# One core, FFT mixing then swish MLP: closing block ordered per output part, first filter group over two queues, evacuations of `a`, `y` and tables shared out

## Chip, cores, metric

One core of a Trainium2 chip. The metric is the device time of one execution in microseconds (us) in the undisturbed ("fast") state, with a granted TensorE clock of 0.998 to 1.0. The profiled span is shorter than the device time of the same execution, by 2.05 us in the first trace and by 1.76 to 3.37 us over all executions; so part of the scatter of device times lies outside the span (one execution of e7 took 785.17 us with a span of 781.8).

## The reference

```python
X = np.fft.rfft(x, axis=1)                         # x: (8, 3008, 256)
Y = X * (filt_r + 1j * filt_i)[None]               # filters: (1505, 256)
x = np.fft.irfft(Y, n=3008, axis=1).reshape(-1, 256)   # 24064 tokens
h = x @ w_in                                       # 256 -> 2048
out = (h / (1 + np.exp(-beta * h))) @ w_out        # 2048 -> 256
```

## The kernel before

The FFT is factored (3008 = 47 x 64) into matmuls with tables that are made on the chip. Sequence 0 is transformed in the set-up (up to 36 us); the seven others are transformed in *units* placed between the steps of the MLP. A step is one filter block of one block of 512 tokens: the h matmul, the activation `gT` on ScalarE, and two steps later the `acc` matmuls. A *turn* of `a` is six transposes into one PSUM tile and their evacuation; an *inner unit* reads `a` back, multiplies it by the filter on VectorE and transforms it on. `S`, `NK`, `NFB` are 3008, 24 and 16. The parts that matter:

```python
def evac(dst, src, on_act, scale=None):            # PSUM -> SBUF
    if on_act: nc.scalar.activation(dst, src, ACT.Copy, ...)
    else:      nc.vector.tensor_copy(dst, src)     # cut

FG = [(g * KG, KG) for g in range(NG)]             # four groups of six filter rows
for h in range(2):                                 # group 0 on POOL's queue, right behind x
    for f, at in ((filt_r, 0), (filt_i, M)):
        load_filter(fri, f, at, *FG[0], gp)[h]()
for part in FG[1:]:                                # the others on SP's queue
    ...

def turn_a(i, on_act):                             # six transposes into one PSUM tile, then one evacuation
    pb = opsum.tile([P, 3, D], BF16, name="pb", tag="acc")
    for e in range(3):
        for dc in range(NDC):
            nc.tensor.transpose(pb[:, e, dc * P : (dc + 1) * P], a_t[...], ident[:])
    evac(a2s[-1][:, 3 * (i % 2) : 3 * (i % 2) + 3, :], pb[:], on_act)
turn_a(0, False); turn_a(1, True)

# placing of units over the steps (place(first, last, units, per step))
place(2, 14, uz(1, True)); place(15, 29, uz(2))    # turns and y of groups 1 and 2
units = uz(3, True); place(20, 24, units[:2], per=2); place(34, 58, units[2:])
at = place(25, 58, u23(1), per=2, gap=2)           # inner units of sequence 1

# closing block: four output parts of 128 tokens, each with its own PSUM tile
todo = [(gT, fb, tb) for tb in range(nch)]
...
on_act = h == 0 and i < 6 or last and h % 2 == 0
evac(ost[:, c : c + per, :], a[:], on_act)
eng = nc.scalar if last and h >= 2 else nc.sync
store(t0 + h * per * P, per * P, ost[:, c : c + per, :], eng)
```

Of the kernel before, what the change touches and what calls it, by code (L numbers as in the profile page):

```python
# [9 lines left out]
P = 128  # L10
# [3 lines left out]
F32 = mybir.dt.float32  # L14
BF16 = mybir.dt.bfloat16
# [11 lines left out]
M = 64  # L27
H = M // 2
NK = 24
J = 32  # L30
KG = 6
NG = NK // KG
# [7 lines left out]
def kernel(  # L40
# [10 lines left out]
    nc = tc.nc  # L51

    B, S, D = x.shape
# [5 lines left out]
    NDC = D // P  # L59
    NFB = FF // P  # L60
    NP = 2 * N1
    KP = 4 * NK
    TB = 512
# [15 lines left out]
    a2pool = pool("a2pool", 5)  # L79
    pqpool = pool("pqpool", 3)  # L80
    vpool = pool("vpool", 4)
    gpool = pool("gpool", 4)
# [24 lines left out]
    def evac(dst, src, on_act, scale=None):  # L107
        if on_act:
            nc.scalar.activation(dst, src, ACT.Copy, scale=1.0 if scale is None else scale)  # L109
        elif scale is None:  # L110
            nc.vector.tensor_copy(dst, src)  # L111
        else:
            nc.vector.tensor_scalar_mul(dst, src, scale)  # L113
# [48 lines left out]
    setup = sp.enter_context(tc.tile_pool(name="setup", bufs=1))  # L162
# [43 lines left out]



    FG = [(g * KG, KG) for g in range(NG)]
    for h in range(2):  # L210
        for f, at in ((filt_r, 0), (filt_i, M)):
            load_filter(fri, f, at, *FG[0], gp)[h]()
    for part in FG[1:]:
        for h in (1, 0):
# [47 lines left out]
    NH = NK // 2  # L262
    us = []
    for h in range(2):
        u = setup.tile([P, NH, M], I32, name="u", tag=f"u{h}")
# [5 lines left out]
        )  # L271
        nc.vector.tensor_scalar(u[:], u[:], TURN - 1, None, ALU.bitwise_and)
        us.append(u)
    rs = [setup.tile([P, NH, M], F32, name="r", tag=f"r{h}") for h in range(2)]

    def t2_part(h, part):
        u, r = us[h], rs[h]
        ks_ = slice(h * NH, (h + 1) * NH)
        if part == 0:
            nc.scalar.activation(  # L280
                t2[:, ks_, 2, :], u[:], ACT.Sin, scale=TWO_PI / TURN, bias=pi[:]
            )
        elif part == 1:
            nc.scalar.activation(r[:], u[:], ACT.Abs, scale=1.0 / TURN, bias=half[:])
        else:
            for cols, sgn, b in ((slice(0, H), -1.0, hp), (slice(H, M), 1.0, hm)):
                nc.scalar.activation(
                    t2[:, ks_, 1, cols], r[:, :, cols], ACT.Sin, scale=sgn * TWO_PI, bias=b[:]
                )
# [104 lines left out]
    a2s = []  # L394

    def turn_a(i, on_act):
        if i % 2 == 0:
            a2s.append(a2pool.tile([P, KG, D], BF16, name="a2", tag="a2"))
        pb = opsum.tile([P, 3, D], BF16, name="pb", tag="acc")
        for e in range(3):  # L400
            k1 = 3 * i + e
            for dc in range(NDC):
                nc.tensor.transpose(
                    pb[:, e, dc * P : (dc + 1) * P],
                    a_t[:, dc, k1, :, :].rearrange("p j a -> p (j a)"),
                    ident[:],
                )
        evac(a2s[-1][:, 3 * (i % 2) : 3 * (i % 2) + 3, :], pb[:], on_act)

    def load_win(h):  # L410
        fs = slice(h * FF // 2, (h + 1) * FF // 2)
# [180 lines left out]
    rest = []  # L592
    for i in range(2 * NDC):
# [1 line left out]
            [P, 4, P], F32, name="ps4", tag="acc" if i % 2 else "f"  # L595
        )
        rest += last_z(0, i, i % 2 == 1, own)
    for go in rest:
        go()

    sp.close()

# [95 lines left out]
    NBLK = (TOK + TB - 1) // TB  # L698
# [4 lines left out]
    def place(a, z, units, clear=False, per=1, gap=0):  # L703
        last_at = a
        for n, go in enumerate(units):
            at = a + (z - a) * n / max(1, len(units) - 1)
            at = max(int(at), last_at + gap if n else last_at)
            if clear and (at % NFB < 2 or at % NFB > 13):
                at += (2 - at) % NFB
            while len(plan.get(at, ())) >= per:  # L710
                at += 1
            plan.setdefault(at, []).append(go)
            last_at = at
        return last_at

    def u1(b, act=False):
        def unit(i):
            def go():
                if i == 0:
                    start(b)  # L720
                s1(b, i, act and i % 2 == 1)

            return go

        return [unit(i) for i in range(J // 2)]

    def u23(b):
        return [lambda i=i: s23(b, i) for i in range(NK // 2 + VLAG)]
# [4 lines left out]
    def uz(g, act=False):  # L733
        return [lambda i=i: turn_z(g, i) for i in range(2)] + [
            lambda i=i: last_z(g, i, act) for i in range(2 * NDC)
        ]
# [21 lines left out]

        return [go]

    place(2, 14, uz(1, True))
    place(15, 29, uz(2))
    units = uz(3, True)
    place(20, 24, units[:2], per=2)
    place(34, 58, units[2:])
# [2 lines left out]
    if B > 1:  # L768
        units = u1(1, True)
        place(3, 8, units[: J // 4], per=2)  # L770
        place(10, 10, uf(0, JG), per=9)
        at = place(9, 14, units[J // 4 :], per=9)
        place(at + 1, at + 1, [lambda: a2_read(1)] + uf(JG, NK), per=9)
        place(14, 20, ut(4), per=2)
        at = place(25, 58, u23(1), per=2, gap=2)
        assert at < 60
        place(60, 60, [lambda: zz_read(1)], per=9)
        place(67, 79, u4(1), per=2)
    if B > 2:
        place(36, 36, ux(2), per=9)  # L780
        at = place(54, 68, u1(2, True), per=3)
        assert at < 75
        place(75, 75, [lambda: a2_read(2)], per=9)
    for b in range(2, B):
        a = first_step[b - 1]
# [32 lines left out]
                c0 += n  # L818

    blk = {}  # L820
    LAG = 2
    for s in range(len(steps) + LAG):
        if s < len(steps):
            i, fb = steps[s]
            t0 = i * TB
            tn = min(TB, TOK - t0)
            hps = hpsum.tile([P, TB], F32, name="hps", tag="hps")
            pos = t0
            while pos < t0 + tn:
                b, n0 = divmod(pos, S)  # L830
                ln = min(S - n0, t0 + tn - pos)
                if s == 0:
                    ln = min(ln, CLS - n0 % CLS)
                for dc in range(NDC):
                    nc.tensor.matmul(  # L835
                        hps[:, pos - t0 : pos - t0 + ln],
                        lhsT=win_sb[:, dc, fb * P : (fb + 1) * P],
                        rhs=ys[b][:, dc, n0 : n0 + ln],
                        start=(dc == 0),
                        stop=(dc == NDC - 1),  # L840
                    )
                pos += ln
            gT = gpool.tile([P, TB], BF16, name="gT", tag="gT")
            nc.scalar.activation(  # L844
                gT[:, :tn], hps[:, :tn], ACT.Silu, scale=beta_sb[:, fb : fb + 1]
            )
            blk[s] = gT
        if s in plan:
            for go in plan[s]:
                go()  # L850
        if s >= LAG:
            i, fb = steps[s - LAG]
            t0 = i * TB
            tn = min(TB, TOK - t0)
            nch = tn // P
            gT = blk.pop(s - LAG)

            last = i == NBLK - 1
            if fb == 0 and not last:
                acc = [opsum.tile([P, 2, D], F32, name="acc", tag="acc") for _ in range(2)]  # L860
            elif fb == 0:
                acc = [
                    (fpsum if h % 2 else opsum).tile(
                        [P, 1, D], F32, name="acc", tag="f" if h % 2 else "acc"
                    )
                    for h in range(nch)
                ]
            per = acc[0].shape[1]


            todo = [(gT, fb, tb) for tb in range(nch)]
            if fb == 0:
                todo, late = todo[: nch // 2], todo[nch // 2 :]
            elif fb == 1:
                todo[nch // 2 : nch // 2] = late
            for g_, f_, tb in todo:
                nc.tensor.matmul(  # L877
                    acc[tb // per][:, tb % per, :],
                    lhsT=g_[:, tb * P : (tb + 1) * P],
                    rhs=wout_sb[:, f_, :],  # L880
                    start=(f_ == 0 and tb % per == 0),
                    stop=(f_ == NFB - 1),
                    skip_group_check=True,
                )
            if fb == NFB - 1:
                for h, a in enumerate(acc):
                    if h * per % 2 == 0:
                        ost = ostp.tile([P, 2, D], F32, name="ost", tag="ost")
                    c = h * per % 2
                    on_act = h == 0 and i < 6 or last and h % 2 == 0  # L890
                    evac(ost[:, c : c + per, :], a[:], on_act)
                    eng = nc.scalar if last and h >= 2 else nc.sync
                    store(t0 + h * per * P, per * P, ost[:, c : c + per, :], eng)


# [28 lines left out]
```

## Time and profile before

| | device time |
|---|---|
| median of 3 | 783.36 us (781.89 to 783.63) |
| the profiled execution | 784.25 us, span 782.2 us |

The page and the chain of waits are in the prediction. One more stretch is needed later: the timeline of the kernel before at the first turn of `a`. Columns of a timeline: start, duration, engine, line, operation, output<-input, shape, count, and in brackets the idle time of the engine ahead of it and what ended it.

```profile
15.32 0.84 PE L403 MATMUL pb<-ident,a_t 128*128 128x128 bf16 x12
15.67 0.64 ACT L287 ACTIVATE t<-r,hm 128x384 bf16<-128x384 f32 x1
15.86 0.56 DVE L111 COPY a<-pb 128x768 bf16<-128x768 bf16 x1 [0.60 <-PE pb L403]
16.20 0.81 ACT L109 ACTIVATE a<-pb 128x768 bf16<-128x768 bf16 x1
16.47 0.38 PE L446 MATMUL ps<-a,t 128*128 128x256 bf16 x2 [0.31 <-DVE a L111]
16.90 0.87 ACT L109 ACTIVATE t<-pt 128x128 bf16<-128x128 bf16 x2
20.08 0.38 PE L472 MATMUL psz<-t,pb_t 128*128 128x128 bf16 x4 [0.21 <-ACT a L109]
```

Twelve transposes (two turns) run in one go; VectorE takes the first turn whole, ScalarE the second, and the first product follows 0.80 us after ScalarE's table step from `hm` has started. Call the start of that step **hm**, the first `psz` matmul **psz**. From hm to psz ScalarE has one thing after another to do: 4.41 us.

### The profile page before, as it was taken

How to read it: one execution, taken by the hardware profiler on the slowest of the kernel's cores; microseconds unless marked ns; L12 is line 12 of the kernel's file. 1: busy time of each engine (PE TensorE's matmuls, PEld its weight loads, DVE VectorE, ACT ScalarE, POOL GpSimd, SP SyncE). 2: the span in 40 equal slices, each digit the busy share in tenths (PEclk: the TensorE clock that was granted, in tenths of full speed). 3: DMA queues.
4: the chain of work that ended last, by engine and by line, in shares of the span. 5: the costliest groups of instructions: out<-in, count | busy, mean ns of one | idle time of the engine just before them, and what ended most of it. 6: DMA issues, size and time to landing. Idle time of an engine off the chain costs nothing.

```text
span 782.2 us, 15445 instructions
## 1 busy us (share of the span) xinstructions
PE 766.8 (98%) x6012; PEld 548.4 (70%) x6108; DVE 393.0 (50%) x644; ACT 594.5 (76%) x921; POOL 142.5 (18%) x145
## 2 busy tenths in 40 slices
PE   8999999999999999999999999999999999999997
PEld 5867667766777666876668766787677776776664
DVE  7847846646446563474636746277453751401001
ACT  6887887886678867787677876778767787677775
POOL 6522501320013100231002410034000430000000
PEclk9999999999999999999999999999999999999999
DMA  9978663517801286022941248312451114100101
GB/s 184 248 186 229 157 210 132 137 58 206 218 28 68 86 205 181 28 95 92 199 154 47 77 132 186 126 67 77 137 180 55 48 68 128 55 28 32 51 28 54
DMA packets 84185, 91.46 MB, mean 117 GB/s; under 512 B 4498, under 2 KB 74276, under 8 KB 83154
## 3 DMA queue, kind: packets, MB, share of 16 engines
q1 hardware_dynamic: 81008, 73.95, 30.7%
q0 software_dynamic: 2816, 16.26, 10.6%
q8 instruction: 48, 0.79, 0.4%
q10 hardware_dynamic: 288, 0.26, 0.1%
q14 instruction: 25, 0.20, 0.1%
HBM read 57.16 MB, written 46.66 MB: 133 GB/s over the span
## 4 chain that ended last, share of the span: by engine, by line
PE 94%; DVE 1%; ACT 1%; issue 1%; DMA 1%; POOL 0%; DVEq 0%; POOLq 0%
PE acc L877 43%; PE hps L835 38%; PE ps L626 3%; PE ps L551 3%; PE ps L674 2%; PE ps L648 2%; DMA xg<-in_x_dram 1%; PE psz L472 0%; DVE q_t L660 0%; ACT a L109 0%; PE pz L543 0%; DVE q_t L663 0%; DVE qb_t L455 0%; DVE p_t L659 0%; ACT a_t L109 0%
## 5 line engine op out<-in xcount | busy, mean ns | idle before, releaser
L844 ACT ACTIVATE gT<-hps,beta_sb 128x512 bf16<-128x512 f32 x752 | 516.0, 687 | 173.5 <-PE hps L835 152.1
L877 PE MATMUL acc<-wout_sb,gT 128*128 128x256 bf16 x3008 | 451.4, 272 | 3.0
L835 PE MATMUL hps<-y,win_sb 128*128 128x512 bf16 (+8 forms) x1636 | 427.4, 350 | 0.5 <-ACT gT L844 0.3
L877 PEld LDWEIGHTS <-gT 128*128 128x128 bf16 x3008 | 285.7, 98 | 128.1 <-ACT gT L844 0.2
L835 PEld LDWEIGHTS <-win_sb 128*128 128x128 bf16 x1730 | 165.0, 98 | 24.7 <-issue 0.6
L664 POOL TENSOR_TENSOR v_t<-p_t,q_t 128x512 bf16<-128x512 f32 x84 | 106.6, 1269 | 387.8 <-DVE q_t L663 381.6
L111 DVE COPY ost<-acc 128x512 f32<-128x512 f32 (+1 forms) x88 | 56.2, 677 | 192.8 <-PE acc L877 188.8
L111 DVE CAST a<-ps 96x512 bf16<-96x512 f32 x96 | 65.9, 687 | 86.2 <-PE ps L626 85.7
L113 DVE TENSOR_SCALAR y<-ps 128x376 bf16<-128x376 f32 (+1 forms) x119 | 63.8, 544 | 61.2 <-PE ps L551 61.2
L659 DVE TENSOR_TENSOR p_t<-ps,frr 128x512 f32<-128x512 f32 x84 | 58.1, 691 | 30.0 <-PE ps L648 28.0
L663 DVE TENSOR_TENSOR q_t<-ps,fri 64x512 f32<-64x512 f32 x84 | 58.3, 694 | 1.2
L660 DVE SCALAR_TENSOR_TENSOR q_t<-ps,fri 64x512 f32<-64x512 f32 x84 | 57.5, 684 | 1.1
L551 PEld LDWEIGHTS <-zz 96*128 96x128 bf16 x512 | 35.3, 97 | 28.9
L109 ACT ACTIVATE z<-ps 128x512 bf16<-128x512 f32 x84 | 49.5, 589 | 0.1
L626 PE MATMUL ps<-xg,t 94*96 94x512 bf16 x112 | 41.9, 381 | 0.7
L551 PE MATMUL ps<-t,zz 96*128 96x94 bf16 x448 | 36.7, 204 | 1.1
L674 PE MATMUL ps<-v_t,t 128*128 128x256 bf16 x168 | 32.1, 273 | 0.6 <-DVE q_t L663 0.6
L648 PE MATMUL ps<-a,t 128*128 128x256 bf16 x168 | 32.1, 273 | 0.1
L120 POOL DMA_DIRECT2D xg<-in_x_dram x22 | 12.1, 551 | 100.8 <-PE acc L877 96.8
L648 PEld LDWEIGHTS <-t 128*128 128x128 bf16 x168 | 15.8, 98 | 14.4
L626 PEld LDWEIGHTS <-t 94*96 94x96 bf16 x112 | 13.6, 123 | 11.9
L674 PEld LDWEIGHTS <-t 128*128 128x128 bf16 x168 | 16.1, 98 | 7.4 <-DVE q_t L663 1.3
(118 smaller groups left out, 191.6 us busy)
## 6 DMA issues: line engine op xcount, KB each, us to landing
out_dram<-ost SPq DMA_DIRECT2D x80, 256.0 KB
d<-a SPq DMA_DIRECT2D x28, 384.0 KB
a<-d SPq DMA_DIRECT2D x28, 384.0 KB
d<-z SPq DMA_DIRECT2D x28, 384.0 KB
zz<-d SPq DMA_DIRECT2D x28, 384.0 KB
xg<-in_x_dram POOLq DMA_DIRECT2D x6, 1280.0 KB, 10.1
frr<-in_filt_r_dram SPq DMA_DIRECT2D x12, 256.0 KB
out_dram<-ost SPq DMA_DIRECT2D x18, 128.0 KB
```

The source lines that it names most:

```text
L111: nc.vector.tensor_copy(dst, src)
L113: nc.vector.tensor_scalar_mul(dst, src, scale)
L551: nc.tensor.matmul(ps[:, e, :NP], lhsT=zz[:, jj + e, dc * P : (dc + 1) * P], rhs=tab[:], start=True, stop=True,)
L626: nc.tensor.matmul(ps[:KP], lhsT=t1[:], rhs=s["x"][:, 2 * i : 2 * i + 2, :], start=True, stop=True)
L648: nc.tensor.matmul(ps[:, e, :], lhsT=t2[:, k0 + e, 3:5, :].rearrange("p c k -> p (c k)"), rhs=s["a2"][g][:, kk + e, :], start=True, stop=True,
L659: nc.vector.tensor_tensor(p_t[:], ps[:], frr[:, ks_, :], ALU.mult)
L663: nc.vector.tensor_tensor(q_t[:M], ps[M:P], fri[M:P, ks_, :], ALU.mult)
L664: nc.gpsimd.tensor_tensor(v_t[:], p_t[:], q_t[:], ALU.add)
L674: nc.tensor.matmul(ps[:, e, :], lhsT=t3[:, k0 + e, :], rhs=v_t[:, e, :], start=True, stop=True)
L835: nc.tensor.matmul(hps[:, pos - t0 : pos - t0 + ln], lhsT=win_sb[:, dc, fb * P : (fb + 1) * P], rhs=ys[b][:, dc, n0 : n0 + ln], start=(dc ...
L844: nc.scalar.activation(gT[:, :tn], hps[:, :tn], ACT.Silu, scale=beta_sb[:, fb : fb + 1])
L877: nc.tensor.matmul(acc[tb // per][:, tb % per, :], lhsT=g_[:, tb * P : (tb + 1) * P], rhs=wout_sb[:, f_, :], start=(f_ == 0 and tb % per = ...
```

## The change

The intent: let the first product start earlier (split evacuation, split filter load), fill two small waits of TensorE, and let only one of four output parts be stored after the last matmul.

```diff
-    FG = [(g * KG, KG) for g in range(NG)]
+    FG = [(0, 2), (2, KG - 2)] + [(g * KG, KG) for g in range(1, NG)]
@@ turn_a, inside the loop over e, after the transposes of one e
-        evac(a2s[-1][:, 3 * (i % 2) : 3 * (i % 2) + 3, :], pb[:], on_act)
+            if i == 0 and e > 0:
+                ks_ = slice(0, 2) if e == 1 else slice(2, 3)
+                evac(a2s[-1][:, ks_, :], pb[:, ks_, :], e == 2)
+        if i > 0:
+            evac(a2s[-1][:, 3 * (i % 2) : 3 * (i % 2) + 3, :], pb[:], on_act)
@@ units
-    for go in rest:
-        go()
-    place(2, 14, uz(1, True))
-    place(15, 29, uz(2))
+    place(0, 0, rest, per=9)
+    place(1, 14, uz(1, True))
+    place(15, 29, uz(2, True))
-        at = place(25, 58, u23(1), per=2, gap=2)
+        units = u23(1)
+        place(20, 53, units[: NK // 2], per=2)
+        at = place(55, 58, units[NK // 2 :], per=2)
-        at = place(54, 68, u1(2, True), per=3)
+        at = place(52, 66, u1(2, True), per=3)
@@ closing block (gT of its last seven filter blocks kept in other pools: cut)
+            if last and fb >= NFB - 7:
+                kept += todo[nch // 2 :]
+                todo = todo[: nch // 2]
+                if fb == NFB - 1:
+                    kept.sort(key=lambda e: e[2])
+                    todo = kept[:4] + todo + kept[4:]
-                    on_act = h == 0 and i < 6 or last and h % 2 == 0
+                    on_act = h == 0 and i < 6 or last and h in (0, 3)
-                    eng = nc.scalar if last and h >= 2 else nc.sync
+                    eng = nc.scalar if last and h == 2 else nc.sync
```

Cut too: the set-up tile `r` becomes a single buffer.

More of the change, by code (lines that the diff above doesn't have):

```diff
@@ L273 @@
         us.append(u)
-    rs = [setup.tile([P, NH, M], F32, name="r", tag=f"r{h}") for h in range(2)]
+    r = setup.tile([P, NH, M], F32, name="r", tag="r")
     def t2_part(h, part):
-        u, r = us[h], rs[h]
+        u = us[h]
         ks_ = slice(h * NH, (h + 1) * NH)
@@ L820 @@
     blk = {}
+    kept = []
     LAG = 2
@@ L842 @@
                 pos += ln
-            gT = gpool.tile([P, TB], BF16, name="gT", tag="gT")
+            if i == NBLK - 1 and NFB - 7 <= fb < NFB - 3:
+                gT = vpool.tile([P, TB], BF16, name="gT", tag="v_t")
+            elif i == NBLK - 1 and NFB - 3 <= fb < NFB - 1:
+                gT = a2pool.tile([P, KG, D], BF16, name="gT", tag="a2")
+                gT = gT[:, :NDC].rearrange("p a d -> p (a d)")
+            else:
+                gT = gpool.tile([P, TB], BF16, name="gT", tag="gT")
             nc.scalar.activation(
```

## The prediction

> **What bounds the kernel now.** The time before is 783.36 us (median of 3, 781.89 to 783.63); the profiled span is 782.2 us. I read the page's busy shares and chain first, then the chain in order of time, then the timeline where the chain leaves TensorE.
>
> ```profile
> PE 766.8 (98%) x6012; PEld 548.4 (70%) x6108; DVE 393.0 (50%) x644; ACT 594.5 (76%) x921; POOL 142.5 (18%) x145
> ...
> PE 94%; DVE 1%; ACT 1%; issue 1%; DMA 1%; POOL 0%; DVEq 0%; POOLq 0%
> ```
>
> TensorE carries 94% of the chain. Its busy share alone says little, because matmuls overlap, so I took starts instead: in the main loop a 128x512 matmul starts 0.217 us after the one before it, a 128x256 one 0.109 us. Adding columns / 2.4 GHz + 2.5 ns over all matmul starts, every gap above this rate after 33 us is either exactly one 512-column matmul (a missing record) or one of these: 0.35, 0.22, 0.10, 0.14 and 0.15 us between 33 and 36 us, 0.51 at 37.3, 0.48 at 75.0, 0.45 at 85.2 and 0.06 at 112. From 113 us to the last matmul at 776.4 TensorE never waits, but for 0.24 us at the very end. The change leaves the number of matmuls alone (6,108 in both programs). So only three stretches can give anything: the set-up up to 37 us, the two waits near 75 and 85 us, and the tail.
>
> The set-up, from the chain in order of time:
>
> ```profile
> 15.30 1.01 ACT t L287 x2
> 16.31 0.70 ACT a L109
> 17.01 0.76 ACT t L109 x2
> 17.77 0.85 ACT t3b L109 x2
> 18.62 1.42 ACT a L109 x2
> 20.08 0.61 PE psz L472 x8
> ```
>
> ScalarE runs from 11.65 to 20 us without a gap, and each of its evacuations frees a PSUM buffer that TensorE wants. From 20.08 to 30.7 us TensorE itself has no gap, and VectorE's products follow it at the same pace. A shift of ScalarE before 20 us therefore shifts everything behind it.
>
> The waits of TensorE after the set-up, from the timeline:
>
> ```profile
> 37.31 0.59 PE L835 MATMUL hps<-y,win_sb 128*128 128x512 bf16 x2 [0.34 <-ACT gT L844]
> ...
> 75.03 0.39 PE L674 MATMUL ps<-v_t,t 128*128 128x256 bf16 x2 [0.32 <-DVE q_t L663]
> ...
> 85.22 0.39 PE L674 MATMUL ps<-v_t,t 128*128 128x256 bf16 x2 [0.28 <-DVE q_t L663]
> ```
>
> The first waits for the first activation, the other two for VectorE to finish reading a PSUM buffer (its product of the unit just before).
>
> The tail, from the timeline:
>
> ```profile
> 776.40 0.66 ACT L109 ACTIVATE ost<-acc 128x256 f32<-128x256 f32 x2 [0.38 <-PE acc L877]
> 776.51 0.76 DVE L111 COPY ost<-acc 128x256 f32<-128x256 f32 x2 [11.88 <-PE acc L877]
> 777.09 2.40 ACTq L796 DMA_DIRECT2D out_dram<-ost  x2
> ```
>
> All four output parts finish within 0.33 us (the last four matmuls start 776.08 to 776.42). The second store on ScalarE's queue is issued at 777.53 but takes 1.96 us to issue; its data lands at 780.7 to 781.22, and the span ends 0.97 us later.
>
> **What the Trainium skill says.** "Perfetto Trace Analysis", Identifying the Most-Contended Engine, warns that matmul occupancy is no measure of how near TensorE is to its limit; the trace agrees (98% busy, weight loads 70%), hence the start-to-start reading. "TensorE: Matmul & The Clock Gate", Back-to-back issue gap, gives N/2.4 + 2.5 ns (216 ns at N = 512) for an isolated matmul and 131 ns sustained; this trace has 217 ns in a sustained stream, so the first form holds here. "DMA: Bandwidth & Descriptors", Anatomy of one DMA, puts about 2 us of fixed cost on a DMA, mostly the receipt of the write; the last stores here land 1.6 to 1.9 us after issue on fifteen of sixteen engines, and 3.5 to 3.7 us on the sixteenth. "Runtime: NRT & Kernel Launch", Instruction fetch mechanics, says instructions come in 16 KiB blocks over a DMA queue; the trace has 48 such packets, the last from 777.7 to 779.1 us, just before the sixteenth engine delivers and while the slow store is being issued.
>
> **The change, part by part.**
>
> *First turn of a.* The first evacuation (128x768, VectorE, 0.56 us) becomes 128x512 on VectorE plus 128x256 on ScalarE. VectorE may begin two transposes earlier (2 x 0.056 = 0.11 us) and is shorter by about a third of its streaming part (estimate 0.13 us), so the first product can come some 0.25 us earlier. But ScalarE gets one more instruction in its gapless stretch. A 128x256 evacuation there costs 0.38 us, at a pitch of 0.28 us (the two at 776.40 and 776.68). The second product needs the table evacuated after it (TensorE waited for that at 17.82), so 20.08 becomes about 20.36: **+0.28 us**.
>
> *Filter group 0.* Before, its four loads on POOL's queue landed at 14.40, 15.21, 15.99 and 16.85 us, just ahead of the first product at 17.03. Without the split the earlier product would meet the load. Now a third of the bytes follow x (landing estimate 14.9: 1.1 us for 256 KB at the measured 3.04 us for 768 KB after x at 13.81), the rest starts on SP at 12.4. Total bytes are the same, so the rest should land near 17.1, before the second product at about 18. **0 us**, enabling only. Groups 1 to 3 keep their place in the byte stream.
>
> *Rest of y after the first activation, group 1's turn one step earlier.* In the order of the changed program eight transposes (8 x 0.056 = 0.45 us) now stand where TensorE waited 0.51 us at 37.31; 0.06 stays. The 128x240 evacuation on ScalarE moves between the first two activations (estimate 0.26 us of pitch), so the fourth step waits about 0.2 us. 0.51 becomes 0.26: **-0.25 us**.
>
> *Units of sequence 1 spread and y of group 2 on ScalarE.* The inner units stood every 2 to 3 steps from step 25; they now stand every 3 steps from step 21. One unit costs VectorE 0.69 + 0.68 + 0.69 = 2.06 us, a step about 1.1 us, so each unit is read before the next wants its buffer; four 0.55 us evacuations leave VectorE too. ScalarE has room: 6.5 to 8.4 of 10 us busy between 50 and 80 us, and back-to-back activations start every 0.58 to 0.65 us. Both waits should go: **-0.93 us**.
>
> *But the first unit now comes early.* It reads the transposed data of sequence 1:
>
> ```profile
> 54.67 0.31 SPq L631 DMA_DIRECT2D d<-a  x1
> ...
> 57.99 1.77 SPq L638 DMA_DIRECT2D a<-d  x4
> ```
>
> The last store of the transposition is issued at 54.67, the reads at 57.99; the first tile's sixteenth increment comes at 61.24. Nothing in that chain moves. In TensorE time the unit stands 23.89 + 0.43 us after the first h matmul (column sums of the changed program); 36.2 + 0.3 + 24.3 = 60.8. The data comes at 61.3: **+0.5 us**. Late in the stretch (steps 53 to 56), units, sequence 2's first matmuls and evacuations crowd the same three PSUM buffers; the dependences show margins of about 0.1 us: **+0.1 us**.
>
> *Tail.* Holding back half of the products of the last seven filter blocks lets the last h matmuls run at ScalarE's pace (about 0.69 us a step instead of 0.87, five steps), then twelve products follow the last activation instead of four. The work is the same; the waits (0.24 before, about 0.4 after) nearly cancel, so TensorE ends where it did. But parts 0, 1, 2 end 1.2, 1.1 and 0.76 us before the last matmul, so their evacuations and stores run beside it. Only part 3 is left: matmul, 0.3 us to ScalarE, which first issues part 2's store (0.40 us), so evacuation from +0.5 to +0.9 us, store issued on SP at about +0.9, that is at 777.3 instead of 777.53. On undisturbed engines it lands 1.75 us later (779.1), on the one busy with the instruction fetch until 779.1 at about 780.3 to 780.9 instead of 781.22. **-0.6 us** (0 to -2).
>
> Sum: 0.28 + 0 - 0.25 - 0.93 + 0.5 + 0.1 - 0.6 = -0.9; 783.36 - 0.9 = **782.5 us**.
>
> **Rivals.**
> 1. *The early unit eats the gain.* If the transposed data comes later than 61.3, each late microsecond stands in TensorE's queue one to one. SP's queue is in order and crowded there (eight loads behind). For: nothing speeds this chain. Against: step 21, not 20, since two units already fill step 20. It would give 783 to 784.
> 2. *The instruction fetch decides the tail.* If it still falls on the last store, the tail gives nothing: 783.1. If the store's packets avoid it, landing at 779.1 gives -2: 781.1.
> 3. *The split turn really gains.* If ScalarE has slack that I do not see, the earlier first product would carry through to 32 us: -0.25 instead of +0.28, total 782.0. The gapless chain speaks against it.
>
> **Range and chances.** The path effects are each below 1 us; runs of one kernel alone differ by 1.7 us. Low end 780.9: best tail, no early-unit wait; high end 784.0: rival 1 with an empty tail. A change of 2% is 15.7 us; no stretch offers that, and none of the added waits could lose it. Faster by over 2%: 0.01; within 2%: 0.98; slower: 0.01.
>
> **What would show it.** First psz matmul at 20.3 to 20.4 rather than 20.08; the first h matmul later by as much; no 0.5 us wait after the second h step; a new wait of the first unit's weight load or matmul for the read-back near 61; no wait for VectorE products at 70 to 90; matmul work ending near the same time, and the last store's issue under 0.5 us. I am wrong if the set-up ends earlier, if a wait over 1 us appears near 61 or 95, or if anything between 120 and 760 us changes.

## The result, and the profile after

| | before | after |
|---|---|---|
| median | 783.50 us (6 runs, 781.89 to 783.79) | 783.49 us (6 runs, 783.42 to 784.04) |
| ratio | | 1.0005, interval 0.9992 to 1.0018: same |

A ratio here compares one kernel's fast runs with the other's fast runs of the same rounds, and is not exactly the ratio of the medians or of the means (e5: 1.0013, by the means 1.0017). The page of the changed kernel, busy times and chain:

```profile
PE 772.4 (99%) x6108; PEld 548.5 (70%) x6108; DVE 390.8 (50%) x640; ACT 595.8 (76%) x926; POOL 142.9 (18%) x145
...
PE 95%; ACT 2%; DVE 1%; DMA 1%; issue 0%; DVEq 0%; ACTq 0%; POOL 0%; POOLq 0%; SPq 0%
```

TensorE carries the chain as before. The six further microseconds of busy PE are no change: the first trace has 6,012 matmul records, this one all 6,108. VectorE has four instructions fewer and ScalarE five more, as the change intends. Now the same stretch as shown for before, in the timeline of the changed kernel:

```profile
14.82 0.62 ACT L287 ACTIVATE t<-r,hm 128x384 bf16<-128x384 f32 x1
14.88 0.42 DVE L111 COPY a<-pb 128x512 bf16<-128x512 bf16 x1 [1.02 <-PE pb L403]
15.35 0.61 PE L403 MATMUL pb<-ident,a_t 128*128 128x128 bf16 x8 [0.51 <-DVE a L111]
15.66 1.15 ACT L109 ACTIVATE a<-pb 128x256 bf16<-128x256 bf16 x2 [0.21 <-PE pb L403]
15.80 0.38 PE L451 MATMUL ps<-a,t 128*128 128x256 bf16 x2
16.70 0.87 ACT L109 ACTIVATE t<-pt 128x128 bf16<-128x128 bf16 x2
19.88 0.38 PE L477 MATMUL psz<-t,pb_t 128*128 128x128 bf16 x4 [0.21 <-ACT a L109]
```

Three things stand here. psz is earlier in absolute time (19.88, not 20.08), but hm is earlier still (14.82, not 15.67): from hm to psz it is 5.06 us, 0.65 more. TensorE's fifth transpose waits 0.51 us for VectorE: the last third of the turn goes into the *same PSUM tile* as the part that VectorE is reading. And the row of 1.15 us on ScalarE is two evacuations (the 128x256 part, then the next turn's 128x768) where before there was one. The first product, for whose sake all this was done, starts 0.98 us after hm (15.80 - 14.82); before it was 0.80.

Where the schedule of the units was changed, the timeline of the changed kernel near 61 and 76 us:

```profile
61.29 0.39 PE L651 MATMUL ps<-a,t 128*128 128x256 bf16 x2 [0.32 <-DMA a<-d]
...
75.05 0.59 ACT L109 ACTIVATE ost<-acc 128x512 f32<-128x512 f32 x1
75.08 0.33 PE L556 MATMUL ps<-t4b,zz 96*128 96x94 bf16 x4
...
75.53 0.69 ACT L857 ACTIVATE gT<-hps,beta_sb 128x512 bf16<-128x512 f32 x1
75.89 0.38 PE L651 MATMUL ps<-a,t 128*128 128x256 bf16 x2
76.10 0.49 ACT L109 ACTIVATE y<-ps 128x376 bf16<-128x376 f32 x1
...
76.65 0.39 PE L677 MATMUL ps<-v_t,t 128*128 128x256 bf16 x2 [0.37 <-ACT y L109]
```

The wait for the read-back of sequence 1 is there, as predicted (0.49 us by the starts of the matmuls). The wait for VectorE at 85 us is gone, the one at 75 is not gone: it has turned into a wait for ScalarE. `y` of group 3 is ready at 75.4 (matmul L556), but ScalarE first evacuates an output part (75.05) and makes a `gT` (75.53), and the next inner unit needs the PSUM buffer that `y` is in: 0.53 us.

The tail, in the timeline of the changed kernel:

```profile
774.46 2.49 PE L897 MATMUL acc<-wout_sb,gT 128*128 128x256 bf16 x20
775.79 0.38 ACT L109 ACTIVATE ost<-acc 128x256 f32<-128x256 f32 x1 [0.38 <-PE acc L897]
775.90 0.76 DVE L111 COPY ost<-acc 128x256 f32<-128x256 f32 x2 [11.21 <-PE acc L897]
776.20 1.78 SPq L802 DMA_DIRECT2D out_dram<-ost  x3
776.68 0.37 ACTq L802 DMA_DIRECT2D out_dram<-ost  x1
777.24 0.38 ACT L109 ACTIVATE ost<-acc 128x256 f32<-128x256 f32 x1 [1.07 <-PE acc L897]
```

And in the timeline of the kernel before, in a second trace of it (a comment line moves its lines by one), because the first is not typical, as the next section shows:

```profile
774.55 1.61 PE L878 MATMUL acc<-wout_sb,gT 128*128 128x256 bf16 x12
775.87 0.66 ACT L110 ACTIVATE ost<-acc 128x256 f32<-128x256 f32 x2 [0.37 <-PE acc L878]
775.98 0.76 DVE L112 COPY ost<-acc 128x256 f32<-128x256 f32 x2 [11.88 <-PE acc L878]
776.28 0.82 SPq L797 DMA_DIRECT2D out_dram<-ost  x2
776.56 0.88 ACTq L797 DMA_DIRECT2D out_dram<-ost  x2
```

In the changed kernel three parts are evacuated or under way when the last matmul (776.68) starts, and one store is left; before, the first evacuation begins as the last matmul starts (775.87 and 775.89), and all four stores come after it.

### The profile page after: what moved, and what is told of

It reads as the page before. It is cut to its first block, busy times and chain, and to the rows that moved or that the text cites. A ratio compares the mean times of both kernels' runs of the same rounds, so it can differ in the third digit from the quotient of the medians.

```text
span 781.4 us, 15550 instructions
## 1 busy us (share of the span) xinstructions
PE 772.4 (99%) x6108; PEld 548.5 (70%) x6108; DVE 390.8 (50%) x640; ACT 595.8 (76%) x926; POOL 142.9 (18%) x145
## 4 chain that ended last, share of the span: by engine, by line
PE 95%; ACT 2%; DVE 1%; DMA 1%; issue 0%; DVEq 0%; ACTq 0%; POOL 0%; POOLq 0%; SPq 0%
PE acc L897 41%; PE hps L842 41%; PE ps L629 3%; PE ps L556 3%; PE ps L677 2%; PE ps L651 2%; PE psz L477 1%; ACT a L109 0%; DMA a<-d 0%; DMA d<-a 0%; ACT gT L857 0%; PE pb L403 0%; ACT a_t L109 0%; ACT t L280 0%; ACT r L284 0%
## 5 line engine op out<-in xcount | busy, mean ns | idle before, releaser
L842 PE MATMUL hps<-y,win_sb 128*128 128x512 bf16 (+8 forms) x1730 | 447.7, 351 | 0.0
L113 DVE TENSOR_SCALAR y<-ps 128x376 bf16<-128x376 f32 (+1 forms) x115 | 61.6, 543 | 58.8 <-PE ps L556 58.8
L556 PEld LDWEIGHTS <-zz 96*128 96x128 bf16 x512 | 35.3, 97 | 29.1 <-issue 0.3
L556 PE MATMUL ps<-t,zz 96*128 96x94 bf16 x448 | 36.7, 204 | 0.0
```

The source lines that it names most:

```text
L113: nc.vector.tensor_scalar_mul(dst, src, scale)
L556: nc.tensor.matmul(ps[:, e, :NP], lhsT=zz[:, jj + e, dc * P : (dc + 1) * P], rhs=tab[:], start=True, stop=True,)
L842: nc.tensor.matmul(hps[:, pos - t0 : pos - t0 + ln], lhsT=win_sb[:, dc, fb * P : (fb + 1) * P], rhs=ys[b][:, dc, n0 : n0 + ln], start=(dc ...
```

## The experiments

All stages of all traces in one table, so that the experiments can be read against each other. *x* is when the last of sixteen increments of the load of x came; *hm* as above; *h* the first h matmul; *513th* and *last* the accumulating matmuls of that number; *stored* the last increment of the last store. The stages sum to the span.

| trace | x | hm | hm to psz | psz to h | h to 513th | 513th to last | last to stored | stored to end |
|---|---|---|---|---|---|---|---|---|
| before | 13.81 | 15.67 | 4.41 | 15.85 | 139.71 | 600.78 | 4.80 | 0.97 |
| before, second (e4) | 11.76 | 14.88 | 4.39 | 15.78 | 140.06 | 600.78 | 3.12 | 0.98 |
| after | 11.82 | 14.82 | 5.06 | 16.04 | 139.78 | 600.98 | 3.37 | 1.35 |
| after, second (e9) | 13.26 | 15.48 | 5.07 | 16.17 | 139.78 | 600.98 | 3.56 | 1.35 |
| e1 tail only | 11.91 | 14.72 | 4.39 | 15.78 | 139.99 | 600.98 | 2.64 | 0.98 |
| e2 schedule only | 12.02 | 14.72 | 4.39 | 15.78 | 141.11 | 600.78 | 3.13 | 0.98 |
| e3 set-up only | 13.23 | 15.51 | 5.07 | 16.05 | 140.60 | 600.78 | 3.14 | 1.31 |
| e5 filter only | 13.58 | 15.81 | 4.40 | 16.36 | 140.80 | 600.78 | 3.14 | 1.22 |
| e6 after, whole turn | 13.25 | 15.47 | 4.40 | 16.12 | 139.75 | 600.98 | 4.05 | 1.34 |
| e7 after, turn last | 12.04 | 14.83 | 4.78 | 16.04 | 139.26 | 600.98 | 2.65 | 1.35 |
| e8 first attempt | 13.14 | 15.46 | 4.40 | 16.12 | 139.74 | 600.98 | 2.65 | 1.35 |
| e11 after, whole filter | 13.11 | 15.05 | 5.06 | 15.77 | 140.05 | 600.98 | 3.38 | 0.97 |
| e10 second attempt | 13.29 | 15.43 | 4.40 | 15.77 | 138.85 | 600.98 | 2.64 | 0.97 |
| e12 third attempt | 11.99 | 14.87 | 4.39 | 15.78 | 138.87 | 600.97 | 3.04 | 0.97 |

My theory when I began: the set-up and the schedule give and take, the tail gains, and x's landing is chance. Its rivals: the split filter load makes x land sooner; the instruction fetch decides the tail; the schedule gains what I had predicted.

### e4, the kernel before again

No edit but a comment line. The two accounts, (a) and (b), of why x seemed to land sooner after the change are put in full under e3.

> The kernel before, unchanged. It gives the noise: runs between 781.9 and 784.3 us. And a second trace of it: account (a) of the early x expects the last of x at 13.8 us again, with ScalarE's transformation with hm at 15.6 to 15.7 us; account (b) lets x land at about 11.9 us and psz start near 19.2 us. For the tail: if the fetch packet of the eighth queue within the last 5 us belongs to this program it is there again, and the stretch from last accumulating matmul to the end is 5.5 to 6 us.

Measured: 782.79 us median (782.1 to 783.45, 5 runs), ratio 0.9999 (0.9985 to 1.0012). x landed at 11.76, psz came at 19.27. So account (b): in the first trace of the kernel before one of sixteen increments of x came 1.8 us behind the others (11.99, then 13.81), here 0.02 us behind. Over all traces x lands near 12 in six and after 13 in eight, with and without the change. The tail was not as I expected: 4.10 us from the last matmul to the end, not 5.5 to 6, although a packet of the instruction queue does lie late in the trace (774.74 us). The first trace, with 5.77, was the exception, and my prediction of the tail had taken it for the rule.

### e1, tail only

```diff
+ the closing-block part of the change; nothing else
```

> The kernel before with the closing block's part of the change alone. Theory (mechanism of the tail right): between the start of the last accumulating matmul and the end of the span 4.7 us instead of 5.8, because only part 3's store comes after the last matmul; TensorE itself ends 0.2 us later; the time falls by about 0.8 us, to some 782.5, if the fast runs of the kernel before average 783.3. Rival (instruction fetch decides the tail): a fetch packet of the eighth queue again falls within the last 5 us and holds one of sixteen engines, the stretch is 5.5 us or more and the time does not fall.

Measured: 781.96 us median (781.45 to 782.86), ratio 0.999 (0.9977 to 1.0002). TensorE from the 513th to the last accumulating matmul 600.98 us, against 600.78: the reordering costs 0.20 us in every trace that has it and in none that hasn't. From the last matmul to the last byte stored 2.64 against 3.12 us: 0.48 gained. So 0.28 us net, by the trace; in the device time a gain is likely, not certain. The stretch to the end is 3.62, shorter than the 4.7 that I had put up: that number had come from the after trace, where one engine was 0.72 us late. The 0.48 us are what undisturbed engines give: of the nine traces with the new tail four have 2.64 or 2.65 us in this column, and in the five others (3.04 to 4.05, both traces of the changed kernel among them) one engine was late in the last stores; of the five traces without the new tail four have 3.12 to 3.14. A packet of the instruction queue in the last 5 us was not seen; it came at 780.53, after the end.

### e2, schedule only

```diff
+ rest, uz(1), uz(2), u23(1), u1(2) placed as in the change; nothing else
```

> The kernel before with the schedule alone (rest of y and its tables placed one step earlier, y of group 2 on ScalarE, inner units of sequence 1 spread). Theory: it gains 0.5 us near 37 and 85 us and loses as much: a wait of 0.3 to 0.5 us for the read-back near 61 us, and one of about 0.5 us for ScalarE's y near 76 us; TensorE's last matmul within 0.2 us of the kernel before, counted from its first h matmul; time within 0.3 us. Rival (my prediction): no wait at 75 to 86 us, last matmul 0.6 us sooner after the first h matmul.

Measured: 782.92 us median (781.69 to 784.02), ratio 0.9999 (0.9987 to 1.0012). By the starts of the matmuls the waits are 0.06 and 0.19 at 36 to 37 us, 0.54 at 61.6, 0.53 at 77.0, 0.18 at 84.5, as the theory had them, and no wait for a product of VectorE at 75 to 86. But from the first h matmul to the last it is 1.05 us longer than in e4, not within 0.2, because of two more waits, in the timeline of this kernel:

```profile
46.60 0.60 PE L624 MATMUL ps<-xg,t 94*96 94x512 bf16 x2 [0.94 <-DMA xg<-in_x_dram]
...
52.21 0.38 PE L624 MATMUL ps<-xg,t 94*96 94x512 bf16 x1 [0.48 <-DVE a L111]
```

The first waits for the last piece of x of sequence 1, which came at 46.47 us here and between 44.50 and 45.67 in e1, e4 and after. That the schedule does it is unlikely: e10 and e12 have the same early steps and no such wait, e5 has the old ones and one of 0.95 us. The second wait is in no other trace; its cause stays open.

### e3, set-up only

```diff
+ split FG, split first turn of a, single r; nothing else
```

> The kernel before with the set-up alone (filter group 0 in two parts over two queues, first turn of a evacuated by VectorE and ScalarE). Theory: from the start of ScalarE's transformation of x with hm to the first set-up product with psz 5.06 us instead of 4.41 (0.34 for one more evacuation, 0.31 for a transpose that waits for VectorE's evacuation of the other part of the same PSUM tile). Two accounts of why psz did not start later all the same: (a) splitting the filter load lets x land about 1 us sooner, then ScalarE's transformation starts near 14.8 us here too; (b) x landed late in the one trace of the kernel before by chance (one slow DMA engine), then it starts at 14.8 or at 15.7 us here, with no relation to the change, and psz starts 0.65 us after the time that the kernel before has with the same landing.

Measured: 783.18 us median (782.36 to 784.5), ratio 1.0005 (0.9993 to 1.0018). hm to psz 5.07, expected 5.06. x landed late (13.23), hm was at 15.51 and psz at 20.58: account (b). Against the first trace of before, hm is 0.16 us earlier and psz 0.50 us later. And two columns that I had not looked at are longer here than in e1, e2 and e4: psz to h (16.05) and stored to end (1.31).

### e9, the changed kernel again

> The changed kernel, unchanged, for a second trace and for its times on the same chip as the other three. If x lands as in the first trace of it (last at 11.8 us) psz is at 19.9 and the first h matmul at 35.9; if one slow engine delays x by 1.5 us, psz is at 20.6 or later, as in the run of the set-up alone. The tail of the first trace had one of sixteen engines 0.73 us late in the last store; without it the stretch from last accumulating matmul to the end is 3.6 to 4.0 us, not 4.7. Time within 0.5 us of the kernel before.

Measured: 783.72 us median (783.5 to 784.94), ratio 1.0011 (0.9998 to 1.0024). x late, psz at 20.55, the first h matmul at 36.72: as expected for that case. In the tail the expectation missed: one engine was 0.92 us behind again, and 4.91 us passed to the end. Its mean is 783.97 us against 782.98 us of the kernel before on the same chip; by the medians it is 0.88 us longer, not within 0.5.

### e6, whole first turn, all else as changed

```diff
-            if i == 0 and e > 0: ...
-        if i > 0:
-            evac(...)
+        evac(a2s[-1][:, 3 * (i % 2) : 3 * (i % 2) + 3, :], pb[:], on_act)
```

> The changed kernel with the first turn of a evacuated whole by VectorE again, all else as changed. Theory (the split turn costs 0.9 us of set-up whatever x does): from the start of ScalarE's second transformation with hm to psz 4.39 us as in three traces without the split (5.06 with it), from psz to the first h matmul 15.78 us (16.04 with it), so the first h matmul comes 0.92 us earlier after the same landing of x. Rival: the split turn needs to be there because the other evacuation comes too late for the first product, then these stretches stay at 5.06 and 16.04. How much of the 0.92 us reaches the end is open: the read-back of sequence 1 lands near 61.2 to 61.5 us whatever the set-up does, so the wait near 61 us may grow from 0.49 to some 1.4 us and eat it; if it does, the time equals that of the changed kernel within 0.3 us, else it is 0.9 us lower.

Measured: 782.87 us median (781.83 to 784.02), ratio 1.0000 (0.9987 to 1.0012), where the changed kernel has 783.72 us in the same rounds. hm to psz 4.40: undoing the split gives 0.67 us back. psz to h stays at 16.12: that half of the theory (16.04 to 15.78 with the turn) falls, it is something else. The device time is 0.85 us lower by the medians, so the gain does reach the end. The cleanest pair is e6 and e9, in which x landed at the same time (13.25 and 13.26): the first h matmul comes 0.74 us earlier and the last accumulating matmul 0.77 us earlier in e6. My expectation that the read-back lands near 61.2 to 61.5 us whatever the set-up does was wrong: it lands 24.8 to 26.7 us after the first h matmul in all traces, at 60.09 to 63.30 us. The wait for it is 0.92 us in e6 against 0.49 in the first after trace, though the first h matmul starts at about the same time (35.98 and 35.92) and the data comes at about the same time (61.27 and 61.24). Two fifths of a microsecond that the after trace loses on the way, 0.26 of it in a wait for ScalarE at 42 us which e6 does not have, are waited here at 61: this wait takes up what is gained between the first h matmul and it, but not what the set-up gains.

### e7, shared evacuation after all six transposes

```diff
+        if i == 0:
+            evac(a2s[-1][:, 0:2, :], pb[:, 0:2, :], False)
+            evac(a2s[-1][:, 2:3, :], pb[:, 2:3, :], True)
```

> The changed kernel with the shared evacuation of the first turn issued after all six transposes, so that no transpose waits for VectorE's part, but ScalarE still has its one more instruction. Theory: of the 0.67 us by which the stretch from hm to psz grew (4.39 to 5.06), 0.34 is the instruction and 0.31 the wait, so here 4.7 us. Rival 1 (the instruction costs it all, the wait is hidden): 5.06. Rival 2 (the wait costs it all): 4.39.

The timeline of this kernel at the first turn:

```profile
14.51 0.79 PE L403 MATMUL pb<-ident,a_t 128*128 128x128 bf16 x11 [0.35 <-ACT a_t L109]
14.83 0.63 ACT L287 ACTIVATE t<-r,hm 128x384 bf16<-128x384 f32 x1
15.00 0.42 DVE L111 COPY a<-pb 128x512 bf16<-128x512 bf16 x1 [1.12 <-PE pb L403]
15.46 1.08 ACT L109 ACTIVATE a<-pb 128x256 bf16<-128x256 bf16 x2
15.48 0.38 PE L450 MATMUL ps<-a,t 128*128 128x256 bf16 x2 [0.18 <-DVE a L111]
```

The transposes run through without the wait, ScalarE goes on at 15.46 without idling, the first product starts 0.65 us after hm (0.80 in the kernel before, 0.98 in the changed one). hm to psz 4.78, expected 4.7. So of the 0.67 us, 0.28 are the wait for the shared PSUM tile and 0.39 the further instruction: its pitch (15.457 to 15.737) is 0.28, as predicted, and it starts 0.63 us after hm where the turn before the change started after 0.52; the earlier first product is real at last and gains nothing, because ScalarE sets psz. Device time 782.29 us median (781.78 to 785.17), ratio 0.9997 (0.9981 to 1.0012).

### e5, filter split only, and e11, changed kernel with the filter whole

```diff
- FG = [(g * KG, KG) for g in range(NG)]
+ FG = [(0, 2), (2, KG - 2)] + [(g * KG, KG) for g in range(1, NG)]
```

e5 is this on the kernel before, e11 the reverse on the changed kernel.

> The kernel before with filter group 0 in two parts over two queues, nothing else. My prediction gave this 0. Theory now: it costs 0.6 us that no data needs. Six traces with the split have 16.04 to 16.17 us from the first psz to the first h matmul, four without it 15.78 to 15.85, whether the turn of a is split or not; and five of the six end 1.31 to 1.36 us after the last store has landed, those without 0.97 to 0.99. So here: 4.39 us from hm to psz (no split turn), then 16.05 to 16.12 us to the first h matmul, 1.3 us from the last landing to the end. Rival: these belong to the split turn and to the reordered units that were in the other six, then 15.8 and 0.97 us here.

> The changed kernel with filter group 0 loaded in one part as before, all else (the split turn too) as changed. Theory: 5.06 us from hm to psz (the turn's cost stays), 15.8 us from psz to the first h matmul, 0.97 us from the last landing to the end; 0.6 us below the changed kernel, so about 783.1 where the kernel before has 782.8. Rival (the split load is what lets the split turn pay): the first product waits for the whole group, which landed at 15.0 us in undisturbed traces and at 16.85 in the first one, and hm to psz is longer than 5.06 us.

Measured: e5 783.34 us median (783.04 to 785.29), ratio 1.0013 (0.9999 to 1.0027); e11 783.36 us (782.92 to 783.94), ratio 1.0009 (0.9997 to 1.0022). psz to h is 16.36 in e5 (more than expected: a further wait of some 0.2 us near 32 us) and 15.77 in e11; stored to end 1.22 and 0.97. So the split load by itself lengthens both columns, in either kernel, and taking it out of the changed kernel takes both back. The device time is too coarse to show it: I had expected e11 to be 0.6 us below the changed kernel, but its ratio of 1.0009 lies between the changed kernel's 1.0005 and 1.0011, and the intervals are wider than that. The rival for e11 fell too: hm to psz 5.06, so nothing waits for the whole group. Where the first of the two comes from, first the timeline of e11:

```profile
26.74 0.81 ACT L109 ACTIVATE a<-pb 128x768 bf16<-128x768 bf16 x1 [0.17 <-PE pb L403]
...
27.42 0.50 PE L354 MATMUL pt<-ident,t 128*128 128x128 bf16 x6
...
27.75 0.39 PE L477 MATMUL psz<-t,pb_t 128*128 128x128 bf16 x4
```

Then that of e5:

```profile
26.91 0.81 ACT L109 ACTIVATE a<-pb 128x768 bf16<-128x768 bf16 x1 [0.17 <-PE pb L403]
...
27.77 0.50 PE L354 MATMUL pt<-ident,t 128*128 128x128 bf16 x6
...
28.25 0.38 PE L472 MATMUL psz<-t,pb_t 128*128 128x128 bf16 x4
```

In e11 the six `pt` transposes start while ScalarE still evacuates `a`; in e5 they start 0.05 us after that evacuation has ended (26.91 + 0.81 = 27.72). The order of TensorE's weight loads is the same in e5 and in the kernel before (6,108 of 6,108 by tile and shape). The compiled program, which is not kept with the runs, says the same of the waits: in the kernels with the split `pt` waits for `a<-pb`, in the kernel before for an earlier `z_t<-psz`. By inference, which PSUM buffer a tile gets has changed with the number of filter loads; this is not shown, and why the allocation should depend on it stays open. The other column, stored to end, is explained for the most part by a row of waits that SyncE works off at the end of the program, one semaphore of a load or store after another, in the order 111, 101, 112, 113 and so on to 118, some 0.06 us apart. With four loads more, the last store gets semaphore 113 in all seven traces with the split; without it, 117 in all seven. So six waits of the row are left after the last store instead of two, and the row ends 0.24 us later: 1.22 us in e5 against 0.98. In the six other traces with the split, SyncE, ScalarE or both also make a closing drain of 0.12 to 0.14 us that starts only after POOL's last one; no trace without the split has it, and why it is late there stays open.

### e8, first attempt at a better version

```diff
  (changed kernel, whole turn)
-    place(34, 58, units[2:])                          # y of group 3
+    place(36, 58, units[2:])
-        place(20, 53, units[: NK // 2], per=2)        # inner units of sequence 1
+        place(23, 53, units[: NK // 2], per=2)
```

> An attempt at a version that beats both: the changed kernel with the first turn evacuated whole, the first inner unit of sequence 1 three steps later (23 rather than 20), and the y evacuations of group 3 two steps later (36 rather than 34), so that they do not stand behind the evacuation of an output part on ScalarE. Theory: no wait for the read-back near 61 us and none for ScalarE's y near 76 us, set-up 0.92 us shorter, tail as changed: the last accumulating matmul 739.7 us after the first h matmul where the changed kernel has 740.8, time 1.5 us below the changed kernel. Rival: each wait removed comes back at the next unit, because the later units now stand closer together (2.7 steps instead of 3) and wait for VectorE: last matmul 740.5 us or more after the first h matmul, and the time is within 1 us.

Measured: 782.47 us median (781.87 to 783.1), ratio 0.9992 (0.998 to 1.0005), 1.25 us below the changed kernel. The rival was right on the stage: 740.72 us from the first h matmul to the last. No wait at 61, but this, in its timeline:

```profile
77.22 0.47 ACT L109 ACTIVATE y<-ps 128x376 bf16<-128x376 f32 x1
...
77.75 0.39 PE L672 MATMUL ps<-v_t,t 128*128 128x256 bf16 x2 [0.82 <-ACT y L109]
```

`y` now stood in the same step as an inner unit: 0.99 us instead of 0.53.

### e10, second attempt, and e12, third

```diff
  (kernel before + tail + schedule of the change; turn and filter as before)
-    place(34, 58, units[2:])
+    for at, go in zip((30, 37, 40, 43, 48, 51), units[2:]):   # e12: (30, 38, 41, 44, 49, 52)
+        place(at, at, [go], per=2)
-        place(20, 53, units[: NK // 2], per=2)
+        place(23, 53, units[: NK // 2], per=2)
```

> Second attempt at a version that beats both: the kernel before with the tail, the rest of y one step earlier, y of group 2 on ScalarE and the spread units, but without the two parts of the set-up, the first inner unit of sequence 1 at step 23, and the y evacuations of group 3 at steps 30, 37, 40, 43, 48, 51, each one step after an inner unit and away from the block ends. Theory: hm to psz 4.39 us, psz to first h 15.78, no wait at 61, none over 0.3 us at 74 to 86, last accumulating matmul 739.8 us after the first h matmul (the kernel before 740.5 to 740.9), last store landed 2.65 us after the last matmul and the end 0.97 us later: 1.2 to 1.6 us below the kernel before, ratio 0.998. Rival (as the first attempt: a removed wait comes back at a later unit): 740.7 us, and only the tail's 0.5 us is left.

> The second attempt with the five later y evacuations of group 3 moved one step on (38, 41, 44, 49, 52), that is before an inner unit rather than after one. The second attempt still waits 0.18, 0.40 and 0.18 us at 77, 81 and 84 us for ScalarE's z of the unit just before. Theory: those waits vanish and nothing takes their place away from the ends of a block, so the last accumulating matmul comes 739.1 us after the first h matmul (739.83 there) and the time is 0.7 us below the second attempt. Rival: the next inner unit waits for y, as in the changed kernel near 76 us (0.53), once or more: 739.8 us or longer, no gain.

Measured: e10 780.99 us median (780.11 to 782.57), ratio 0.9981 (0.9968 to 0.9993); e12 781.02 us (780.66 to 781.21), ratio 0.9978 (0.9965 to 0.9992). Both intervals lie below 1 (still "same", which means within 2%): 1.5 and 1.9 us less than the kernel before, by the means. The stages of e10 are where they were expected (first h matmul to last 739.83 us, expected 739.8), but for one wait of 0.40 us at 80.8 where I had put none over 0.3. At 61 us the unit now comes after its data; both in the timeline of e10:

```profile
61.98 0.33 PE L551 MATMUL ps<-t4b,zz 96*128 96x94 bf16 x4
62.15 0.38 PE L646 MATMUL ps<-a,t 128*128 128x256 bf16 x2
...
80.80 0.33 PE L551 MATMUL ps<-t4b,zz 96*128 96x94 bf16 x4 [0.23 <-ACT z L109]
```

e12 was to remove that last one. It did, and 0.12, 0.33 and 0.08 us of other waits came in its place: 739.84 us, the rival.

## Why the prediction was right or wrong

The class (same) and the range (780.9 to 784.0) held; 782.5 was 1.0 us too low. A gain of 0.9 us was predicted, and the measured difference is a loss of 0.4 us, if anything. The range is as wide as the scatter of one kernel, so that it held says little about the mechanism: that was wrong in several terms. Step by step:

- **First turn of `a`, "+0.28 us".** Right in kind: the split loses, because ScalarE has no slack. Mis-sized: 0.67 us (4.40 to 5.07, e6 against e9). The term counted the pitch of one small evacuation (0.28); e7 measures 0.39 for it, and 0.28 more is a wait that I had not seen: the transposes of the last third write into the PSUM tile that VectorE is reading. My line that the first product "can come some 0.25 us earlier" failed for the same reason: it came 0.18 us later. What would have shown it, "first psz at 20.3 to 20.4", seemed refuted by 19.88; it was x's landing that hid it.
- **Filter group 0, "0 us, enabling only".** Wrong: e5 and e11 show 0.27 us between psz and h in the changed kernel (16.04 against 15.77; more in e5), and 0.38 us after the last store. The bytes do land in time in the changed kernel, as I had argued (the rest at 16.26 and 17.90 us in its two traces, VectorE's product with it at 17.42 and 18.09), though only just in e5 (18.22 and 18.34, 0.13 us behind VectorE's pace); it is the program around them that changed.
- **Rest of `y` one step earlier, "-0.25 us".** Right: 0.51 became 0.06 and 0.19.
- **Units spread, "Both waits should go: -0.93 us".** Half. The wait at 85 us went, but 0.18 us for ScalarE stayed; at 75 us the waiting moved from VectorE to ScalarE (0.48 to 0.53). "ScalarE has room" was a mean over 10 us; at a block end it has an output part and a `gT` in line just when `y` comes. With the waits of the first trace that is -0.22 us.
- **First unit ahead of its read-back, "+0.5 us".** Right: 0.49, and 0.43 to 0.95 over the six traces with this placement. It takes up what is gained between the first h matmul and it (0.92 in e6), but the set-up's gain passes, since the read-back moves with the first h matmul; the time fell where rival 1 had put it (783 to 784), but for the most part not for its reason.
- **Crowding, "+0.1 us".** 0.16 us of waits near 98 us.
- **Tail, "-0.6 us (0 to -2)".** In the two first traces it was -1.05 from the last matmul on, but the first of before was out of the ordinary (and in it I had misread the fourth store: its fifteenth increment came 3.31 us after the issue, not 1.6 to 1.9). On undisturbed engines it is -0.48 for the stores and +0.20 for the reordering, which I had let cancel: -0.28. With the late engines counted in, the means of "last to stored" are 3.11 us in nine traces with the new tail and 3.47 in five without, so -0.36 for the stores, of which chance is a large part. Rival 2, that the instruction fetch decides it: in e6 a packet of its queue starts at 778.65 us and one engine is 1.4 us late, but in the two after traces no packet lies in the last 5 us and one engine is 0.72 and 0.92 us late all the same. So something else can make it late; what it is stays open.

The net of these measured terms: +0.67, +0.27 and +0.38 for the set-up and its companion at the end, -0.48 + 0.20 for the tail, and for all units together 139.78 us against 140.06 and 139.71 in the two traces of before, so -0.1 in the mean: +0.9 us. The two comparisons of means gave +0.4 and +1.0 us. Against my sum of -0.9, the set-up makes 1.0 us of the difference, the units 0.5, the tail 0.3. Only the set-up's share is firm. The stage of the units, h to 513th, scatters: 139.71 to 140.80 us in the five traces with the old schedule (mean 140.23), 139.26 to 141.11 in the six with the changed one (mean 139.96); e10 and e12 alone lie clear of both, at 138.85 and 138.87, and there lies most of their gain.

## What to carry to other kernels

By these runs, splitting an evacuation over two engines can help only if the engine that takes the second part has slack there, and if the matmuls that fill the rest do not write into the PSUM tile that the first engine is reading; here both failed. When single traces of the same kernel differ by more than the change is worth, compare stages between fixed events (hm to psz, the 513th matmul to the last): these two agreed to 0.02 us from trace to trace of one kernel, where the times scattered by 2 us, and a load that lands late by chance no longer hides what the change did. A stage with loads of its own (h to 513th) scatters too. A unit moved earlier wants its data looked up first; moved into a step with another that shares its PSUM buffers, it only moves the wait.

## What the Trainium skill lacked or had wrong

- "Perfetto Trace Analysis", Optimization Strategy, tells to find the gaps of the engine and the instruction whose semaphore ends them; that found each wait here. It does not say that a gap may come and go between executions of one program: the wait at 84 to 87 us of the kernel before was 0.45 us in one trace and 0.80 in another.
- "DMA: Bandwidth & Descriptors", Latency and other measured facts, calls two of the sixteen engines usually slower. Here the number changes from execution to execution: of the sixteen increments of the last piece of x, none came more than 0.5 us after the eighth in e4, one in the first trace of the kernel before (1.8 us behind the fifteenth), four in e9. The traces do not show which engine it is.
- No page has it that a change in the number of loads can change which wait a transpose gets, with the order of TensorE's instructions unchanged (0.27 us between psz and h, e11 against after), or which semaphore the last store gets, and so how many of SyncE's closing waits come after it: two, with 0.97 or 0.98 us to the end, or six, with 1.22 to 1.35.
